# First batch of a retention, Fourier and MLP kernel: part of its transforms from float32 to float16 pairs, with a new order written out by hand

## The chip, the cores and the metric

The kernel runs on one core of one Trainium2 chip. The metric is the device time of one execution in microseconds. Before the change it is 596.29 us, the median of 3 runs (596.05 to 597.14).

## What is computed

The reference chains three blocks over x of 2 batches, 768 tokens and 512 features. The first is a retention (linear attention with decay) over 8 heads. The second adds a Fourier mix and an MLP, the third a plain MLP:

```python
X = np.fft.fft(np.fft.fft(x, axis=1), axis=2)          # over tokens, then over features
u = x + np.real(X)
un = (u - mean(u)) / np.sqrt(var(u) + 1e-06)
y = u + np.maximum(un @ w_ch1, 0.0) @ w_ch2            # 512 -> 2048 -> 512
z = y + np.maximum((norm(y) * g_ln) @ w2_ch1, 0.0) @ w2_ch2
```

Inputs and output are float32, but for the weight matrices, which are float64 and unpacked on the chip.

## The kernel before, in words

The two Fourier transforms are matrix products. Symmetry in tokens and features is used first: rows are added to and subtracted from their mirror rows ("folds"), so that a transform needs about a quarter of the products. Tokens lie in tiles `U[b][j]` of 128 tokens and 512 features, j from 0 to 2 for the first half of the sequence and 3 to 5 for its mirror.

Most products are done in float16 pairs: a float32 number is held as a high and a low float16, and a product is three passes (high by high, high by low, low by high: `PASS`). A pair costs a cast on ScalarE for the high half and a subtraction on GpSimd or VectorE for the low half. In the first batch both transforms are kept in float32, which needs no such pair.

The program has four stages. The retention of batch 0 (0 to about 34 us), its transforms, and the normalization and first tiles of the first MLP (34 to about 67 us) are the head. After that the first MLP runs over four blocks of 384 tokens, with batch 1's retention and transforms and the unpacking of weights in the background, and then the second MLP.

The head from 34 us on is ordered by hand. The string `ORDER` is a list of tokens, each one step of a chain of instructions, and the list is emitted in that order on TensorE, VectorE, ScalarE and GpSimd. The tokens that matter here:
- `k0` to `k2`, `j0` to `j2` are the even and odd folds of tile 0, 1, 2 (`fold_half`, L500 to L517, on VectorE);
- `d<m><g>` is the product of fold m with group g of the first transform (`dft1_mm`), of five groups, accumulated over m = 2, 1, 0; `D<g>` takes a group out of PSUM (`dft1_out`, L543);
- `q<j>`, `p<j>` are the sine and the cosine part of the second transform of tile j (`dft2_q`, `dft2_p`); `X<j>` subtracts and adds the sine part (`sub_sin`, L601), `P<j>` adds the cosine part (`add_cos`, L608);
- `R` is a special row: three GpSimd folds, a cast, and a low half on GpSimd (`row_fold`, L418);
- `b<j>`, `n<j>` are the statistics of the normalization and the normalized, transposed tile (`ln_steps`, `ln_pe_steps`); `M<j><f>` is the first MLP product of tile j and output tile f (f = 0 to 2);
- `c<i>` unpacks weight tile i of the first MLP matrix (`conv_steps`, L286); `W<n>` issues n products whose result is not used.

Unpacking a weight tile takes, on the usual path, a ScalarE copy into `top` (L305), a shift on VectorE (L307), an OR on VectorE (L308), a cast to the high half on ScalarE (L321) and a subtraction for the low half on GpSimd (L323). A second path (L296 to L299) uses two ScalarE copies and one VectorE instruction.

After the hand-ordered part a scheduler orders everything. It may put nothing of the following unpacking on VectorE before the last `n` step there: `after("dve", ...)`, L988 to L993. The shifts L307 of that unpacking write to the PSUM buffers that the second transform's results held, so they also need the last reader of those results on ScalarE (`dft2_yp`, L635 and L636). The names of a tile in the rows leave out buffer numbers: `w` is a weight tile, `f` a fold, `ps_h` and `ps_y` the MLP's sums.

Of the kernel before, what the change touches and what calls it, by code (L numbers as in the profile page):

```python
# [19 lines left out]
P = 128  # L20
# [24 lines left out]
c0 S B1 B0 s s B1 B0 s s O4 B1 B0 O4 c0 I O4 R I O5 O5 O5 O5 c0 c1 c2 W12 k2 j2 k2 k2 d24 d20 d21 j2 j2 d22 d23  # L45
k1 k1 k1 d14 d10 d11 j1 j1 j1 d12 d13 c3 j0 j0 j0 d03 k0 k0 k0 d02 c1 D3 R c2 R c0 D2 d04 d01 D4 d00 c3 D1 q0 D0 q0
c1 q2 q2 X0 X0 q1 q1 c2 X1 p0 p1 P0 c1 X1 P1 b0 b1 b0 X2 c3 p2 c2 b0 b1 X2 P2 c3 b0 n0 b1 b2 b1
W27 n0 b2 n1 n0 b2 W6 n1 n0 b2 M00 n2 n1 n2 n2 n1 M01 M12 M11 M10 n2 M22 M20 M02 M21
# [30 lines left out]
def shape_tables():  # L79
    t = np.arange(TB)  # L80
    s = np.arange(NS)
    ang = 2.0 * np.pi * ((t[:, None] * s[None, :]) % S) / S
    cs = np.cos(ang) * TS
    sn = np.sin(ang) * TS
    d = np.arange(P)
    dd = np.arange(ND)
    cd = np.cos(2.0 * np.pi * ((d[:, None] * dd[None, :]) % DM) / DM) * TS
    dse, dso = d[:, None] * dd[None, 2:-1:2], (d[:, None] + 1) * dd[None, 1::2]
    sd = np.sin(2.0 * np.pi * (np.concatenate([dso, dse], 1) % DM) / DM) * TS
    sd[P - 1, :P] *= 0.5  # L90
# [8 lines left out]
    cdp = np.concatenate([cd[:, ::2], cd[:, 1::2]], 1)  # L99
    drow = np.where(dd[::2] % 4, -0.5, 0.5) * TS  # L100
# [7 lines left out]
    return {  # L108
        "cs": lay(cs, 3),
        "sn": lay(sn[:, :TB], 3),  # L110
        "cd": lay(np.concatenate([cd[:, ::2], cd[:, 1::2]], 1), 1)[:, :, 0],
        "sd": lay(sd, 1)[:, :, 0],
        "cr": ((np.where(s % 2, -1.0, 1.0) - 1.0) * TS).astype(np.float16)[None],
        "dr": (np.where(dd[::2] % 4, -0.5, 0.5) * TS).astype(np.float16)[None],
        "cs32": full(cs, 3),
        "sn32": full(sn[:, :TB], 3),
        "cd32": full(cdp, 1)[:, 0],
        "sd32": full(sd, 1)[:, 0],
        "dr32": drow.astype(np.float32)[None],
        "expo": expo,  # L120
    }
# [3 lines left out]
def tile_retention_fourier_mlp(ctx: ExitStack, tc: tile.TileContext, a: dict, out: bass.AP):  # L125
# [98 lines left out]
    def load_tables(b):  # L224
        if b == 0:
            both = const.tile([P, 2 * ND - 2], F32, tag="big3", name="cdsd32")
            cd, sd = both[:, :ND], both[:, ND:]
            rooms = (("cs", [P, 3, NS], "big1"), ("sn", [P, 3, TB], "big2"), ("cd", cd, None), ("sd", sd, None),
                     ("cr", [1, NS], "cr"), ("dr", [1, NE1], "dr32"))
        else:  # L230
            both = const.tile([P, 2, 2 * ND - 2], F16, tag="big3", name="cdsd")
            cd, sd = both[:, :, :ND], both[:, :, ND:]
            rooms = (("cs", [P, 2, 3, NS], "big1"), ("sn", [P, 2, 3, TB], "big2"), ("cd", cd, None), ("sd", sd, None),
                     ("dr", [1, NE1], "dr"))
        for nm, shape, room in rooms:
            src = nm if b or nm == "cr" else nm + "32"
            tab[nm] = const.tile(shape, F16 if src == nm else F32, tag=room, name=f"{nm}_{b}") if room else shape
            sp.dma_start(tab[nm], a[src])
# [47 lines left out]
    def conv_steps(kind, m, i, which=None, into=None):  # L286
# [6 lines left out]
        if m == 1:  # L293
# [207 lines left out]
    def fold_half(b, m, cos, eng=dve):  # L501
        x_, y_ = U[b][m], U[b][3 + m]
        if (b, m) not in folds:
            folds[b, m] = [f32t(f"{nm}{b}_{m}", 13 - 3 * m + i if b == 0 else None) for i, nm in enumerate("eof")]
            fhl[b, m] = hl(f"fhl{b}_{m}") if b else folds[b, m][2]
# [22 lines left out]
    def dft1_mm(b, g, m, ps, first, last):  # L528
        c0, w, tn, n = GRP[g]
        t = tab[tn]  # L530
        f = fhl[b, m]
        if b == 0:
# [10 lines left out]
    def dft1_out(b, g, ps):  # L543
        w, n = GRP[g][1], GRP[g][3]
        if b == 0:
            t = cst[b, g] = csp.tile([P, NS], F32, tag=f"cs{g}", name=f"cst{b}_{g}")
            act.activation(t[:w, :n], ps[:w, :n], AF.Copy, scale=CS)
            yield
            return
# [6 lines left out]
    def dft1_part(b, g, m, ps):  # L556
        cosg = GRP[g][2] == "cs"
        dft1_mm(b, g, m, ps, m == 2, m == 0 and not cosg)
        if cosg and m == 0:
            dft1_row(b, g, ps)  # L560
# [7 lines left out]
    def dft2_p(b, ps, s0, w):  # L568
        for g, o in ((0, slice(0, NE1)), (1, slice(NE1, ND))):
            if b == 0:  # L570
                pe.matmul(ps[:w, o], cst[b, g][:, s0:s0 + w], tab["cd"][:, o], start=True, stop=g == 1)
                if g == 0:
                    pe.matmul(ps[:w, o], cst[b, 4][0:1, s0:s0 + w], tab["dr"], start=False, stop=True)
                continue
# [10 lines left out]
    def dft2_q(b, j, bk):  # L585
# [4 lines left out]
        for g, o, w in parts:  # L590
            for n, (x, y) in enumerate(PASS if b else ()):
                pe.matmul(ps[:, ND + o:ND + o + w], cst[b, g][:, x, j * P:(j + 1) * P], tab["sd"][:, y, o:o + w],
                          start=n == 0, stop=n == 2)
            if b == 0:
                pe.matmul(ps[:, ND + o:ND + o + w], cst[b, g][:, j * P:(j + 1) * P], tab["sd"][:, o:o + w], start=True, stop=True)
# [97 lines left out]
    def ln_pe_steps(m, blk, j, bk):  # L693
# [10 lines left out]
        act.copy(t[:, 0], psv)  # L704
# [254 lines left out]
    for i in range(NE, 4):  # L959
        chains[f"c{i}"] = lambda i=i: conv_steps(1, 0, i, None if i else "at")  # L960
    for j in range(3):
# [125 lines left out]
    for n in range(total + LAG):  # L1087
# [5 lines left out]
        for _, _, task in sorted(bg.pop(n, ()), key=lambda z: z[0]):  # L1093
            after("dve", task) if n < GATEN else task()
# [30 lines left out]
```

## Time and profile before

| | |
|---|---|
| median of 3 runs | 596.29 us (596.05 to 597.14) |
| the profiled execution | 598.83 us, span 597.0 us |
| TensorE busy | 572.3 us, 96% |
| VectorE busy | 396.0 us, 66% |
| ScalarE, GpSimd busy | 277.4 us (46%), 279.3 us (47%) |
| moved by DMA | 63.23 MB |

The span is what the profile's rows cover, and the execution's time has 1.83 us around it. PE is TensorE, PEld its weight loads, DVE VectorE, ACT ScalarE, POOL GpSimd, SP SyncE, which issues transfers. A busy PE is not PE at its peak, since instructions overlap in its pipeline. The granted clock (PEclk) reads 1.00 at 2.4 GHz and 0.50 at 1.2 GHz.

### The profile page before, as it was taken

To read this page: it belongs to the slowest core of one execution; us is meant where nothing else is said; L and a number is where in the kernel's file an instruction comes from. 1 tells how busy PE (TensorE), PEld (TensorE's weight loads), DVE (VectorE), ACT (ScalarE), POOL (GpSimd) and SP (SyncE) were. 2 spreads that over 40 slices of the span, in tenths; PEclk is the share of its full clock that TensorE was granted. 3 is DMA by queue.
4 is the path that set the end of the run, shared out by engine and by line. 5 is a ranking of instruction groups with operands and counts; after the bars stand their busy time and mean duration, and the time that the engine had idled before them with its cause. 6 is when DMAs were issued, how large, how long until landed. Compare 5 with 4: busy or idle time off the path is not lost. (4 is left out here: it accounts for less than half of the span.)

```text
span 597.0 us, 11805 instructions
## 1 busy us (share of the span) xinstructions
PE 572.3 (96%) x4629; PEld 375.9 (63%) x4629; DVE 396.0 (66%) x869; ACT 277.4 (46%) x557; POOL 279.3 (47%) x294
## 2 busy tenths in 40 slices
PE   7889999989999999999998999999999999999997
PEld 4746645555644554677766666676777677767773
DVE  6897898764695599886597559666545553555333
ACT  3646789643223433454478786864223222322110
POOL 8926889966353575442359776764111200110000
PEclk9999999999999999999999999999999999999999
DMA  8994269842000110353154552510210025002001
GB/s 285 410 414 167 89 201 345 271 154 72 1 1 0 24 31 1 85 146 124 37 163 142 173 175 91 167 27 2 63 27 19 1 85 58 19 1 87 21 2 53
DMA packets 46327, 63.23 MB, mean 106 GB/s; under 512 B 26177, under 2 KB 28351, under 8 KB 46271
## 3 DMA queue, kind: packets, MB, share of 16 engines
q1 hardware_dynamic: 45598, 62.40, 33.0%
q8 instruction: 36, 0.59, 0.4%
q10 hardware_dynamic: 672, 0.08, 0.1%
q14 instruction: 21, 0.16, 0.1%
HBM read 52.23 MB, written 6.29 MB: 98 GB/s over the span
## 5 line engine op out<-in xcount | busy, mean ns | idle before, releaser
L866 PE MATMUL ps_y<-w,h 128*128 128x512 f16 x1152 | 280.6, 380 | 3.4 <-ACT h L851 1.5
L866 PEld LDWEIGHTS <-h 128*128 128x128 f16 x1152 | 109.4, 98 | 105.4 <-issue 4.2
L819 PEld LDWEIGHTS <-sw 128*128 128x128 f16 x1104 | 94.4, 98 | 15.8 <-issue 1.9
L819 PE MATMUL ps<-th,sw 128*128 128x192 f16 x828 | 92.1, 246 | 1.6 <-DVE wf L299 1.3
L323 POOL TENSOR_TENSOR w<-wf,w 128x512 f16<-128x512 f32 x58 | 67.8, 1176 | 39.1 <-ACT w L321 38.9
L819 PEld LDWEIGHTS <-w 128*128 128x128 f16 x828 | 71.9, 98 | 19.0 <-issue 0.6
L851 ACT ACTIVATE h<-ps 128x384 f16<-128x384 f32 x92 | 43.5, 490 | 69.5 <-DVE ps L845 65.8
L726 PE MATMUL ps_h<-unT,w 128*128 128x384 f16 x396 | 73.7, 326 | 1.7 <-DVE h L741 1.6
L819 PE MATMUL ps<-unT,w 128*128 128x192 f16 x552 | 62.7, 246 | 0.0
L726 PEld LDWEIGHTS <-w 128*128 128x128 f16 x396 | 37.0, 98 | 29.8 <-issue 3.1
L852 DVE SCALAR_TENSOR_TENSOR h<-ps,h 128x384 f16<-128x384 f32 x92 | 49.0, 553 | 8.3 <-ACT h L851 6.7
L771 POOL TENSOR_TENSOR sw<-ws,sw 128x512 f16<-128x512 f32 x32 | 38.0, 1198 | 32.8 <-ACT sw L770 32.8
L839 DVE TENSOR_TENSOR t<-ps,s 128x192 f32<-128x192 f32 x46 | 16.3, 355 | 49.6 <-PE ps L819 49.5
L831 ACT COPY s<-ps 128x192 f32<-128x192 f32 x46 | 14.5, 316 | 69.9 <-PE ps L819 69.9
L689 POOL TENSOR_TENSOR uns<-un,uns 128x512 f16<-128x512 f32 x21 | 24.6, 1171 | 41.2 <-ACT uns L688 41.2
L795 POOL TENSOR_TENSOR th<-ts,th 128x384 f16<-128x384 f32 x24 | 22.5, 956 | 36.6 <-ACT th L794 36.6
L321 ACT CAST w<-wf 128x512 f16<-128x512 f32 x58 | 35.1, 612 | 9.8 <-DVE wf L308 6.7
L845 DVE TENSOR_TENSOR ps<-ps,s 128x192 f32<-128x192 f32 x46 | 16.6, 362 | 29.2 <-PE ps L819 28.9
L668 POOL TENSOR_TENSOR rs<-rs,neghalf 128x1 f32<-128x1 f32 x24 | 13.1, 548 | 48.0 <-DVE rs L666 48.0
L832 DVE TENSOR_TENSOR s<-ps,s 128x192 f32<-128x192 f32 x46 | 16.2, 352 | 25.6 <-ACT s L831 25.5
L373 POOL TENSOR_TENSOR m<-m,m 128x512 f16<-128x512 f32 x24 | 31.1, 1310 | 2.5 <-ACT m L371 2.5
L299 DVE SCALAR_TENSOR_TENSOR wf<-ws,ps_w 128x512 int32<-128x512 int32 x32 | 21.9, 683 | 15.1 <-ACT ps_w L297 8.3
(166 smaller groups left out, 847.5 us busy)
## 6 DMA issues: line engine op xcount, KB each, us to landing
ws<-in_w SPq DMA_DIRECT2D x25, 511.8 KB, 4.5
ws<-in_w2b SPq DMA_DIRECT2D x16, 511.8 KB, 3.6
ws<-in_w1b SPq DMA_DIRECT2D x16, 511.8 KB, 4.5
kt<-in_kt SPq DMA_DIRECT2D x12, 256.0 KB, 3.6
qt<-in_qt SPq DMA_DIRECT2D x12, 256.0 KB, 5.2
v<-in_v SPq DMA_DIRECT2D x12, 256.0 KB
k<-in_k SPq DMA_DIRECT2D x12, 256.0 KB, 5.7
pre<-in_w SPq DMA_DIRECT2D x4, 511.8 KB
```

What stands on the lines that cost most here:

```text
L299: dve.scalar_tensor_tensor(ti, raw[:, :, 0], 13, part.bitcast(I32), op0=ALU.logical_shift_right, op1=ALU.bitwise_or)
L321: act.copy(hi, t)
L323: (dve if m == 0 and i in (LD1 if kind == 1 else LD2) else pool).tensor_tensor(lo, t, hi, op=ALU.subtract)
L373: pool.tensor_tensor(t[:, 1], m32, t[:, 0], op=ALU.subtract)
L689: pool.tensor_tensor(s_[:, 1], un, s_[:, 0], op=ALU.subtract)
L726: pe.matmul(ps, w[:, i, k, fo:fo + P], x[:, j, k, :], start=n == 0, stop=n == 11)
L771: pool.tensor_tensor(lo, z, hi, op=ALU.subtract)
L795: pool.tensor_tensor(t[:, 1], z, t[:, 0], op=ALU.subtract)
L819: pe.matmul(ps, lhs, rhs, start=start and n == 0, stop=n == 5, skip_group_check=True)
L851: act.activation(hi, z, AF.Relu)
L852: dve.scalar_tensor_tensor(lo, z, 0.0, hi, op0=ALU.max, op1=ALU.subtract)
L866: pe.matmul(dn[blk][j], h[:, x, j * P:(j + 1) * P], w[:, y], start=f == 0 and n == 0, stop=f == NF - 1 and n == 2)
```

## The change

In batch 0, the last third of the first transform (m = 0) and the whole second transform are done in float16 pairs. The fold of m = 0 gets a pair (a new step `H`), its first two passes are issued first and the third as a step of its own (`l<g>`), `D<g>` makes a pair with a new VectorE instruction, and `q` and `p` take three passes. The tables of the second transform are loaded once, in float16, for both batches. Weight tiles 1 to 3 take the unpacking path with two ScalarE copies. The first subtraction of `X1` moves to GpSimd. The `W27` and `W6` become one `W8`. The unpacking behind the head must wait for the last `n` step on ScalarE as well as on VectorE. `ORDER` is new from the folds on.

```diff
 ORDER = """
-k1 k1 k1 d14 d10 d11 j1 j1 j1 d12 d13 c3 j0 j0 j0 d03 k0 k0 k0 d02 c1 D3 R c2 R c0 D2 d04 d01 D4 d00 c3 D1 q0 D0 q0
+k1 k1 k1 d14 d10 d11 j1 j1 j1 d12 d13 j0 j0 j0 k0 k0 k0 H H c1 c2 c3 c1 c2 c3 d03 d02 d04 d01 d00 l3 D3 D3 l2 D2 D2 l4 D4 D4
...
+        for nm, t in (("cs", cs), ("sn", sn)):
+            tab[nm + "32"] = t
+            sp.dma_start(t[:, 1:], a[nm + "32"][:, 1:])
+            t = tab[nm] = t[:, 0].bitcast(F16).rearrange("p (y n) -> p y n", y=2).unsqueeze(2)
+            sp.dma_start(t[:, :, 0], a[nm][:, :, 0])
...
-        if m == 1:
+        if m == 1 or (kind == 1 and i in (1, 2, 3)):
...
+    def fold_split(b, m):
+        f, t = folds[b, m][2], fhl[b, m]
+        act.copy(t[:, 0], f)
+        yield
+        pool.tensor_tensor(t[:, 1], f, t[:, 0], op=ALU.subtract)
+        yield
...
-    def dft1_mm(b, g, m, ps, first, last):
+    def dft1_mm(b, g, m, ps, first, last, part=slice(0, 3)):
...
-        if b == 0:
-            pe.matmul(ps[:w, :n], f[:, c0:c0 + w], t[:, m, :n], start=first, stop=last)
+        if b == 0 and m > 0:
+            pe.matmul(ps[:w, :n], f[:, c0:c0 + w], tab[tn + "32"][:, m, :n], start=first, stop=last)
             return
-        for i, (x, y) in enumerate(PASS):
-            pe.matmul(ps[:w, :n], f[:, x, c0:c0 + w], t[:, y, m, :n], start=first and i == 0, stop=last and i == 2)
+        for i, (x, y) in enumerate(PASS[part]):
+            pe.matmul(ps[:w, :n], f[:, x, c0:c0 + w], tab[tn][:, y, m, :n], start=first and i == 0,
+                      stop=last and part.start + i == 2)
...
-            for n, (x, y) in enumerate(PASS if b else ()):
+            for n, (x, y) in enumerate(PASS):
...
-        dve.tensor_tensor(x_[:, :ND], x_[:, :ND], qs, op=ALU.subtract)
+        (eng if j == 1 else dve).tensor_tensor(x_[:, :ND], x_[:, :ND], qs, op=ALU.subtract)
...
-        act.copy(t[:, 0], psv)
+        gate["act"] = act.copy(t[:, 0], psv)
...
-    after("dve", lambda: [w_conv(2, 0, i) for i in range(2)])
+    after("dve", lambda: after("act", lambda: [w_conv(2, 0, i) for i in range(2)]))
```

Two places show what the new order does. The first is GpSimd, from the special row's low half (`rhl`) to the powers of the normalization (`rs`). `w` is the low half of weight tile 0, 1, 2, 3 in turn, `u` with `qs` a step of `X`, `fhl` the fold's new low half. Line numbers are those of each kernel. Before:

```order
L431 TENSOR_TENSOR rhl_763<-r_653,rhl_763 1x257
L323 TENSOR_TENSOR w_0_0_688<-wf_0_0_578,w_0_0_688 128x512
L323 TENSOR_TENSOR w_0_0_688<-wf_0_1_690,w_0_0_688 128x512
L605 TENSOR_TENSOR u_119<-u_119,qs_198 128x255
L323 TENSOR_TENSOR w_0_0_688<-wf_0_2_692,w_0_0_688 128x512
L605 TENSOR_TENSOR u_119<-u_119,qs_199 128x255
L323 TENSOR_TENSOR w_0_0_688<-wf_0_3_744,w_0_0_688 128x512
L668 TENSOR_TENSOR rs_0_0_832<-rs_0_0_832,neghalf 128x1
```

With the change:

```order
L429 TENSOR_TENSOR rhl_720<-r_655,rhl_720 1x257
L321 TENSOR_TENSOR w_0_0_690<-wf_0_0_580,w_0_0_690 128x512
L521 TENSOR_TENSOR fhl_0_764<-f_0_763,fhl_0_764 128x512
L321 TENSOR_TENSOR w_0_0_690<-wf_0_1_705,w_0_0_690 128x512
L321 TENSOR_TENSOR w_0_0_690<-wf_0_2_710,w_0_0_690 128x512
L321 TENSOR_TENSOR w_0_0_690<-wf_0_3_715,w_0_0_690 128x512
L594 TENSOR_TENSOR u_119<-u_119,qs_198 128x257
L596 TENSOR_TENSOR u_119<-u_119,qs_198 128x255
L659 TENSOR_TENSOR rs_0_0_873<-rs_0_0_873,neghalf 128x1
```

The first two instructions are the same, but the cast that feeds `rhl` now stands on ScalarE ahead of the fold's cast, where before it stood behind the first group taken out of PSUM. The four low halves stand together, and both steps of `X1` follow them on GpSimd.

The second place is ScalarE at the end of the head, from the last transposed tile (`unT`, from `ps_l`) to the first high half of the unpacking behind it (`w`). `cosy` are the cosine results, read out of the PSUM buffers `ps_pq` 0, 1, 2. Before:

```order
L635 ACTIVATE cosy_0_1064<-ps_pq_0_786 128x129
L636 ACTIVATE cosy_0_1064<-ps_pq_0_786 128x128
L635 ACTIVATE cosy_1_1075<-ps_pq_1_801 128x129
L636 ACTIVATE cosy_1_1075<-ps_pq_1_801 128x128
L635 ACTIVATE cosy_2_1080<-ps_pq_2_794 128x129
L636 ACTIVATE cosy_2_1080<-ps_pq_2_794 128x128
L704 CAST unT_0_841<-ps_l_0_2_922 128x4x128
L740 ACTIVATE h_0_0_1030<-ps_h_0_0_905 128x384
L321 CAST w_0_0_1051<-wf_0_0_1046 128x512
```

With the change:

```order
L695 CAST unT_0_887<-ps_l_0_2_1000 128x4x128
L303 ACTIVATE top_189<-ws_0_0_1071 128x512
L303 ACTIVATE top_190<-ws_0_1_1081 128x512
L626 ACTIVATE cosy_0_1091<-ps_pq_0_818 128x129
L627 ACTIVATE cosy_0_1091<-ps_pq_0_818 128x128
L626 ACTIVATE cosy_1_1107<-ps_pq_1_825 128x129
L627 ACTIVATE cosy_1_1107<-ps_pq_1_825 128x128
L626 ACTIVATE cosy_2_1112<-ps_pq_2_832 128x129
L627 ACTIVATE cosy_2_1112<-ps_pq_2_832 128x128
L303 ACTIVATE top_188<-pre_344 128x512
```

The readers of the second transform's buffers stood ahead of the last transposed tile and now stand behind it, with two `top` copies between. Before, those two copies stood far ahead, among the groups of the first transform.

## Rows read from the trace of the kernel before

**Rows 1.** Windows: stretch, length, busy us (instructions) of PE, PEld, DVE, ACT, POOL, PEclk, DMA share, GB/s.

```profile
60.00:70.00 10.00, 8.85 (x123) 7.00 (x121) 7.84 (x15) 6.82 (x18) 8.14 (x11) 1.00 0.29 106
70.00:80.00 10.00, 8.86 (x49) 4.54 (x48) 10.00 (x22) 7.68 (x17) 7.76 (x8) 1.00 0.31 80
80.00:90.00 10.00, 10.00 (x64) 5.50 (x62) 9.80 (x20) 9.91 (x19) 10.00 (x11) 1.00 0.83 258
...
110.00:120.00 10.00, 9.79 (x107) 6.00 (x107) 8.43 (x16) 6.39 (x12) 9.90 (x10) 1.00 0.87 294
120.00:140.00 20.00, 17.63 (x147) 9.95 (x145) 11.80 (x19) 9.09 (x17) 13.03 (x12) 0.91 0.43 136
```

**Rows 2.** Timeline, folds to unpacking: start us, us, engine, line, operation, count, [idle before <-releaser].

```profile
35.98 0.61 ACT L321 CAST w<-wf 128x512 f16<-128x512 f32 x1
...
40.74 0.68 DVE L507 TENSOR_TENSOR o<-u 128x512 f32<-128x512 f32 x1
...
43.72 0.29 DVE L513 TENSOR_TENSOR f<-e 128x129 f32<-128x129 f32 x1
...
45.49 0.67 POOL L431 TENSOR_TENSOR rhl<-r,rhl 1x257 f16<-1x257 f32 x1 [10.78 <-DVE wf L307]
45.58 2.24 DVE L308 TENSOR_TENSOR wf<-wf,top 128x512 int32<-128x512 int32 x1
...
46.12 1.15 POOL L323 TENSOR_TENSOR w<-wf,w 128x512 f16<-128x512 f32 x1
```

**Rows 3.** Timeline, TensorE: the end of the first transform, and the first MLP products.

```profile
42.49 2.74 PE L533 MATMUL ps_d<-sn,f 128*128 128x384 f32 x8
...
48.58 0.50 PE L541 MATMUL ps_d<-cr,rhl 1*128 1x385 f16 x2
...
61.74 5.52 PE L716 MATMUL ps_h<-unT,w 128*128 128x128 f16 x96
```

**Rows 4.** Timeline, second transform to the first shift of the unpacking behind the head.

```profile
50.48 0.43 DVE L603 TENSOR_TENSOR u<-u,qs 128x257 f32<-128x257 f32 x1 [1.53 <-ACT qs L598]
...
52.46 1.40 DVE L613 SCALAR_TENSOR_TENSOR u<-ps_pq,u 128x256 f32<-128x256 f32 x4
...
53.79 1.27 DVE L660 BATCH_NORM_STATS2 bst<-u 128x6 f32<-128x512 f32 x2
...
55.07 1.26 DVE L603 TENSOR_TENSOR u<-u,qs 128x257 f32<-128x257 f32 x1
...
58.16 0.66 PE L701 MATMUL ps_l<-expo,un 128*128 128x128 f32 x4 [1.14 <-ACT un L680]
...
61.57 0.29 ACT L635 ACTIVATE cosy<-ps_pq 128x129 f32<-128x129 f32 x1
...
63.80 1.28 DVE L307 TENSOR_SCALAR ps_w<-ws 128x512 int32<-128x512 int32 x2
```

**Rows 5.** Timeline, the first weight tile behind the head, and TensorE behind it.

```profile
65.58 1.88 DVE L308 TENSOR_TENSOR wf<-ps_w,top 128x512 int32<-128x512 int32 x3
65.96 0.49 ACT L740 ACTIVATE h<-ps_h 128x384 f16<-128x384 f32 x1 [2.80 <-PE ps_h L716]
...
67.04 1.16 POOL L323 TENSOR_TENSOR w<-wf,w 128x512 f16<-128x512 f32 x1 [1.22 <-ACT w L321]
...
69.62 0.55 DVE L741 SCALAR_TENSOR_TENSOR h<-ps_h,h 128x384 f16<-128x384 f32 x1
...
78.76 2.11 PE L726 MATMUL ps_h<-unT,w 128*128 128x384 f16 x12
...
80.71 2.11 PE L866 MATMUL ps_y<-w,h 128*128 128x512 f16 x9
```

**Rows 6.** Timeline of the late stall.

```profile
123.90 0.66 ACT L296 ACTIVATE half<-ws 128x512 f16<-128x512 bf16 x1 [3.48 <-DMA ws<-in_w2b]
...
129.82 0.58 PE L476 MATMUL ps_st<-vhl,khl 128*64 128x64 f16 x24 [1.29 <-DVE int L409]
```

**Rows 7.** Window behind that stall (columns as in rows 1).

```profile
132.00:134.00 2.00, 2.00 (x7) 0.71 (x6) 1.93 (x5) 0.62 (x1) 1.26 (x2) 0.50 0.75 244
```

More of the change, by code (lines that the diff above doesn't have):

```diff
@@ L116, in shape_tables @@
         "sn32": full(sn[:, :TB], 3),
-        "cd32": full(cdp, 1)[:, 0],
-        "sd32": full(sd, 1)[:, 0],
-        "dr32": drow.astype(np.float32)[None],
         "expo": expo,
@@ L224, in load_tables @@
     def load_tables(b):
-        if b == 0:
[L226 to L238, printed above, removed]
+        cs, sn = (const.tile([P, 3, n], F32, tag=f"big{i}", name=f"{nm}_{b}") for i, nm, n in ((1, "cs", NS), (2, "sn", TB)))
+        if b:
+            for nm, t in (("cs", cs), ("sn", sn)):
+                t = tab[nm] = t.rearrange("p k n -> p (k n)").bitcast(F16).rearrange("p (y k n) -> p y k n", y=2, k=3)
+                sp.dma_start(t, a[nm])
+            return
+        for nm, t in (("cs", cs), ("sn", sn)):
+            tab[nm + "32"] = t
+            sp.dma_start(t[:, 1:], a[nm + "32"][:, 1:])
+            t = tab[nm] = t[:, 0].bitcast(F16).rearrange("p (y n) -> p y n", y=2).unsqueeze(2)
+            sp.dma_start(t[:, :, 0], a[nm][:, :, 0])
+        both = const.tile([P, 2, 2 * ND - 2], F16, tag="big3", name="cdsd")
+        tab["cd"], tab["sd"] = both[:, :, :ND], both[:, :, ND:]
+        tab["cr"] = const.tile([1, NS], F16, name="cr")
+        tab["dr"] = const.tile([1, NE1], F16, name="dr")
+        for nm in ("cd", "sd", "cr", "dr"):
+            sp.dma_start(tab[nm], a[nm])
     neghalf = const.tile([P, 1], F32, name="neghalf")
@@ L504, in fold_half @@
             folds[b, m] = [f32t(f"{nm}{b}_{m}", 13 - 3 * m + i if b == 0 else None) for i, nm in enumerate("eof")]
-            fhl[b, m] = hl(f"fhl{b}_{m}") if b else folds[b, m][2]
+            fhl[b, m] = hl(f"fhl{b}_{m}") if b or m == 0 else folds[b, m][2]
         z, f = folds[b, m][1 - cos], folds[b, m][2]
@@ L554, in dft1_out, with dft1_part @@
         yield
-    def dft1_part(b, g, m, ps):
+    def dft1_part(b, g, m, ps, part=slice(0, 3)):
         cosg = GRP[g][2] == "cs"
-        dft1_mm(b, g, m, ps, m == 2, m == 0 and not cosg)
-        if cosg and m == 0:
+        dft1_mm(b, g, m, ps, m == 2, m == 0 and not cosg, part)
+        if cosg and m == 0 and part.stop == 3:
             dft1_row(b, g, ps)
@@ L569, in dft2_p @@
         for g, o in ((0, slice(0, NE1)), (1, slice(NE1, ND))):
[L570 to L574, printed above, removed]
             for n, (x, y) in enumerate(PASS):
@@ L965, in tile_retention_fourier_mlp @@
         chains[f"n{j}"] = lambda j=j: ln_pe_steps(0, 0, j, bk0)
+    chains["H"] = lambda: fold_split(0, 0)
     todo = {"S": lambda: attn_scores(0, 5, bk0)}
+    todo |= {f"l{g}": lambda g=g: dft1_part(0, g, 0, ps1[g], slice(2, 3)) for g in range(5)}
     todo |= {f"d{m}{g}": lambda m=m, g=g: first(g, m) for m in range(3) for g in range(5)}
@@ L997, in tile_retention_fourier_mlp @@
         after("pool", lambda: dft2_y0(0, j))
-    after("dve", lambda: [w_conv(2, 0, i) for i in range(2)])
+    after("dve", lambda: after("act", lambda: [w_conv(2, 0, i) for i in range(2)]))
     for j in range(3):
-        dft2_y(0, j, bk0) if YA[0] == "a" else after("dve", lambda: dft2_y(0, j, bk0))
+        after("act", lambda: dft2_y(0, j, bk0)) if YA[0] == "a" else after("dve", lambda: dft2_y(0, j, bk0))
     NB = 2 * B
@@ L1093, in tile_retention_fourier_mlp @@
         for _, _, task in sorted(bg.pop(n, ()), key=lambda z: z[0]):
-            after("dve", task) if n < GATEN else task()
+            after("dve", lambda: after("act", task)) if n < GATEN else task()
         if n >= LAG:
```

25 lines of the change are left out of this document (6 added, 19 removed).

## The prediction

> **What bounds the kernel now.** I read the windows first, then the timeline of the head, then the waits of the stages behind it. The windows show who is full in which stage [rows 1]. From 70 to 80 us VectorE is busy 10.00 of 10 us and TensorE 8.86: there the unpacking of the MLP's weights sets the pace. From 80 to 90 TensorE is busy 10.00 and so on to 118 us, with 9.79 between 110 and 120. What is still lost behind that lies mostly between 120 and 140 us (17.63 of 20, and a mean granted clock of 0.91). So a change of the head is worth what it does to the moment from which TensorE has no gap, and that moment hangs on the first unpacking instruction behind the head, VectorE's shift at 63.80 us [rows 4]. In the timeline the reader is to see what that shift waits for, which is where the change bites.
>
> **The change, part by part.** I follow the chain from the last fold to that shift.
>
> *Folds.* They end at 44.01 us now (43.72 + 0.29), and GpSimd was idle for 10.78 us before its step on the special row at 45.49 [rows 2]. In the new order this step needs only a ScalarE cast that stands ahead of the fold's cast. ScalarE starts its weight cast at 35.98 (0.61), then has three pairs of copies. The first of a pair took 0.66 [rows 6], the second has no row in the head, and I price it as the cast, 0.61 [rows 2]; three pairs are 3.8 us, so GpSimd starts at about 40.7. Its two instructions (0.67 and 1.15) then run until 42.5, in the middle of the folds, where VectorE works on SBUF operands without a pause (the fold at 40.74 took 0.68). The one place where the trace has such a meeting is 45.58: a VectorE instruction of that size, both inputs in SBUF, took 2.24 us beside exactly these two GpSimd instructions, so 1.56 more than 0.68 [rows 2]. I take 1.6 (bounds 0, if they don't meet, and 1.8, both GpSimd instructions whole). The last fold is then ready at 45.6.
>
> The Trainium skill, "SBUF — State Buffer", section "SBUF: two separate sides", says that VectorE with two SBUF inputs and GpSimd exclude each other for whole instructions. By that rule the term would be 1.8 instead of 1.6 and the sum 0.2 us higher; the measured row decides here.
>
> *First transform, last third.* A float32 product of 384 columns took 0.69 (2.74 for eight records, two to a product) [rows 3]; in float16 twelve of them start 1.95 apart from the next group, so 0.16 each [rows 5], and three passes are 0.49. TensorE gains 0.2 on each of five groups, but first waits for the new cast, 0.61 behind the last fold. Cast done at 46.2; ten products of the first two passes, 1.6; five third passes, 0.8; six products on the special row, 0.215 each (0.43 for the two before 49.01, where the sine part begins), 1.3. The new low half (1.15 on GpSimd) is ready at 47.4, behind the ten products' start and ahead of their end at 47.8, so it costs nothing; if the cover went, it would cost up to 1.15. The transform ends at 49.9, where it was 49.0 now [rows 3].
>
> *Second transform.* The last group leaves PSUM as a pair: by the nearest rows 0.49 on ScalarE and 0.55 on VectorE [rows 5], done at 51.1 with the hand-overs. The sine subtractions of tile 0 are two of 0.43 [rows 4]; now GpSimd does the first half of tile 1 beside them. Such a meeting stretched the same line to 1.26 at 55.07, 0.83 more. I take 0.6 (bounds 0 and 0.83), since a GpSimd instruction of half of 1.15's length is the partner here. Two cosine additions are 0.7 (1.40 for four) [rows 4]: done at 53.3. The sine and cosine products run in this time on TensorE and cost nothing. From the last addition to the first transposes now pass 4.3 us (53.86 to 58.16). I take off the 0.83 of stretch and one of the two statistics (0.64), and add the two additions that the new order puts in between (0.7): 3.5. First transposes at 56.8, **1.3 us earlier than now**.
>
> *To the shift.* The third tile's statistics now stand behind the first tile's low half: 56.8 + 0.66 + a cast 0.61 + 0.69 is 58.8. From statistics to transposes took 4.37 (53.79 to 58.16), less 0.83 and 0.64, so 2.9, and the second tile's low half stands in between, 0.7: third transposes at 62.4, where the trace before shows the last of the tiles done before the shift at 63.80 [rows 4]. Behind them ScalarE has the transposed tile's cast (0.66 + 0.1 + 0.61: 63.8), then two weight copies (0.66 each by rows 6: 65.1), and only then the two readers of the PSUM buffer that the first shift writes (0.29 each, overlapping: 0.46) [rows 4]. **The shift starts at 65.5 instead of 63.80: 1.7 us later.** The removed warm-up products, 33 against 8, were not on this chain.
>
> *Behind the shift.* From the first shift to the first low half in place are 63.80 to 68.20 now [rows 4, 5], so 69.9 then. TensorE's first tiles end earlier than now: 63.1 after the third transposes plus half of the 96 products that took 5.52 [rows 3] is 66, against 67.26. That gain is hidden: TensorE waits for the weights in either case, and VectorE is full behind the shift. So I carry the 1.7 us to 80.71, from where TensorE has no gap [rows 5], and to the end.
>
> *Edits at no cost.* Tiles 1 to 3 need one VectorE instruction instead of two; these stand where VectorE waits for TensorE. Two more table transfers, equal bytes: the folds cover them, and ScalarE reads the weights behind them only from 36.6 on; uncovered they cost two issues of SP. The second transform's tables are not loaded again later: nothing waited for them. The added wait on ScalarE is in the chain above.
>
> **Sum.** The profiled execution takes 598.83 us (span 597.0 and 1.83 around it), and 600.5 with 1.7 more. The median of the runs is 2.54 below the profiled one, so 596.29 + 1.7 = **598.0 us**. A measurement of this kernel can tell about 0.2%, 1.2 us, from no change. With the bounds of the two meetings the forecast's own range is 597.0 to 599.0.
>
> **The rivals.**
>
> *The two engines don't meet* (no change). If GpSimd's steps fall between folds, or wait until the folds are done, and tile 1's half doesn't hold up tile 0's, 1.6 + 0.6 go: the shift at 63.3, 0.5 earlier than now, 595.8 us. For it: the new order does shorten the chain to the transposes. Against it: two meetings in the trace, both with a stretch [rows 2, 4].
>
> *The clock falls* (slower still). With 8 warm-up products for 33, TensorE stands from about 66 to 69.9 with one product in between. At 129.82 it had stood for 1.29 us, worked 0.58 and stood again, and from 132 to 134 the granted clock was 0.50, 1.2 GHz [rows 6, 7]. Two microseconds at half clock are 1.0 lost, the whole drop 1.8 (0.09 of 20 us) [rows 1]. VectorE then waits for the products of output tile 3, so the loss would be passed on: 599.0 to 599.8. It decides if the gap is as long as worked out. The Trainium skill, "TensorE: Matmul & The Clock Gate", Part 1, says that the throttled state is the default and that only activity releases it; by that rule this rival is what happens, and the trace agrees with its 0.50 behind the gap.
>
> *The late stall closes* (faster). Between 120 and 140 us the loss is 2.4 us of idle TensorE and 1.8 of clock, 4.2 together [rows 1]. It comes from one place: ScalarE stood for 3.48 us in front of a weight transfer of the second MLP, with the retention's casts queued behind it [rows 6]. The scheduler gave this stage another order, with one of those copies moved among the casts. If the transfer lands before ScalarE gets there, most of it goes: 598.0 - 3.7 = 594.3. Against it: the transfers hang on the buffers that the same unpacking frees, and that starts later.
>
> **How the numbers follow.** The forecast has 0.40, no meeting 0.20, the clock 0.22, the closed stall 0.18. The range reaches from the closed stall to the clock's upper end, 594.0 to 600.0; about 0.15 is left for the full stall saved on top of the missing meetings and for losses in sum above the clock's. Slower by over 0.2%: the clock and most of the forecast, 0.22 + 0.35 = 0.57. Within 0.2%: no meeting, but for a little, and the forecast's lower end, 0.22. Faster by over 0.2%: the closed stall and what is left, 0.21.
>
> **What would show it.** Right: GpSimd's low half of the special row at about 41 us with a fold beside it of well over 0.68; the last fold at 45.6; the first transposes before 57.5; the first shift behind the head after 65, released by ScalarE's cosine readers; TensorE idle for over 2 us behind the first tiles. Wrong: folds that end at 44.0, a shift before 64.2, or a stretch from 120 to 140 us with TensorE full. A granted clock under 1.00 between 66 and 75 us is the second rival.

## The result, and the profile after

The changed kernel takes 603.21 us (median of 6 runs, 601.32 to 606.13) against 596.51 for the kernel before on the same chip (6 runs): a ratio of 1.0111, 95% interval 1.0091 to 1.0132. It is slower by 6.7 us, where 1.7 were forecast, and lies outside the range (594.0 to 600.0).

| | before | after |
|---|---|---|
| the profiled execution, span | 598.83, 597.0 us | 603.88, 602.1 us |
| last fold ends | 44.01 | 45.49 |
| first, third transposes | 58.16, 61.25 | 56.78, 63.57 |
| first shift behind the head | 63.80 | 66.44 |
| first product on a weight tile from behind the head | 67.10 | 69.61 |
| mean granted clock | 0.996 | 0.993 |

The profiled executions differ by 5.05 us, the medians by 6.7: that of the kernel before lost 1.8 us to the clock behind its late stop [rows 1, 7], which its executions at a mean clock of 0.999 or 1.000 (60 of the 107 in the comparisons below, 594.4 to 597.1 us) didn't lose.

Windows after, columns as in [rows 1]; the lines from 60:70 to 120:140 answer to those:

```profile
58.00:60.00 2.00, 1.89 (x16) 1.81 (x16) 1.63 (x4) 0.77 (x2) 0.13 (x1) 0.59 0.00 0
60.00:62.00 2.00, 2.00 (x22) 1.93 (x21) 0.88 (x2) 0.74 (x2) 2.00 (x4) 0.56 0.00 0
...
60.00:70.00 10.00, 7.56 (x104) 6.87 (x102) 5.13 (x10) 7.08 (x17) 7.65 (x12) 0.91 0.17 54
70.00:80.00 10.00, 8.80 (x52) 4.45 (x52) 10.00 (x21) 7.77 (x16) 7.91 (x8) 1.00 0.17 53
80.00:90.00 10.00, 10.00 (x56) 5.17 (x54) 10.00 (x20) 9.32 (x17) 9.97 (x11) 1.00 0.80 250
110.00:120.00 10.00, 10.00 (x90) 6.11 (x89) 7.02 (x11) 7.69 (x13) 8.92 (x10) 1.00 0.79 290
120.00:140.00 20.00, 17.49 (x171) 10.38 (x170) 14.40 (x25) 9.61 (x18) 13.29 (x13) 0.92 0.57 183
...
220.00:240.00 20.00, 18.73 (x102) 9.86 (x101) 19.19 (x42) 6.55 (x13) 12.29 (x13) 1.00 0.15 14
240.00:260.00 20.00, 17.92 (x130) 11.48 (x129) 15.06 (x33) 9.78 (x19) 8.65 (x10) 1.00 0.33 86
```

The same two late windows of the kernel before, not shown so far:

```profile
220.00:240.00 20.00, 18.38 (x99) 9.53 (x98) 18.04 (x38) 7.65 (x16) 11.80 (x13) 1.00 0.05 10
240.00:260.00 20.00, 20.00 (x156) 13.54 (x155) 17.28 (x37) 9.26 (x18) 7.12 (x7) 1.00 0.44 114
```

Two things meet the eye. The clock falls in the head: the granted share is 0.59 and 0.56 from 58 to 62 us. And far behind the head, where the diff touches nothing, TensorE is idle for 1.27 + 2.08 = 3.35 us between 220 and 260, before for 1.62. The stop between 120 and 140 us is as large as it was.

Timeline after, from the folds to the first warm-up products, which answers to [rows 2, 3]:

```profile
40.56 0.69 POOL L429 TENSOR_TENSOR rhl<-r,rhl 1x257 f16<-1x257 f32 x1 [5.96 <-ACT rhl L427]
40.64 2.27 DVE L505 TENSOR_TENSOR o<-u 128x512 f32<-128x512 f32 x1
41.22 1.14 POOL L321 TENSOR_TENSOR w<-wf,w 128x512 f16<-128x512 f32 x1
...
45.20 0.29 DVE L511 TENSOR_TENSOR f<-e 128x129 f32<-128x129 f32 x1
...
45.52 0.62 ACT L519 CAST fhl<-f 128x512 f16<-128x512 f32 x1 [5.04 <-DVE f L511]
...
46.20 0.82 PE L538 MATMUL ps_d<-sn,fhl 128*128 128x384 f16 x4 [2.35 <-ACT fhl L519]
...
50.10 0.49 PE L544 MATMUL ps_d<-cr,rhl 1*128 1x385 f16 x2
...
51.95 1.02 POOL L594 TENSOR_TENSOR u<-u,qs 128x257 f32<-128x257 f32 x1 [1.23 <-ACT qs L589]
51.97 0.42 DVE L596 TENSOR_TENSOR u<-u,qs 128x255 f32<-128x255 f32 x1
...
52.53 0.76 DVE L604 SCALAR_TENSOR_TENSOR u<-ps_pq,u 128x256 f32<-128x256 f32 x2
...
53.65 1.04 PE L975 MATMUL warm<-expo 128*128 128x256 f16 x8
```

The fold beside GpSimd's step takes 2.27 instead of 0.68, and TensorE stands for 2.35 us in front of the float16 products, where it had float32 work before. In the second meeting, at 51.95, it is GpSimd's step that is stretched (1.02; its next one takes 0.72), and VectorE's takes 0.42.

Timeline after, from the first transposes to the first tiles' end, which answers to [rows 4, 5]:

```profile
56.78 0.66 PE L692 MATMUL ps_l<-expo,un 128*128 128x128 f32 x4 [2.10 <-ACT un L671]
...
58.70 0.69 DVE L651 BATCH_NORM_STATS2 bst<-u 128x6 f32<-128x512 f32 x1
...
60.07 3.66 PE L707 MATMUL ps_h<-unT,w 128*128 128x128 f16 x48
...
61.84 0.82 ACT L671 ACTIVATE un<-u,rs 128x512 f32<-128x512 f32 x1 [0.95 <-DVE rs L670]
...
64.69 1.42 ACT L303 ACTIVATE top<-ws 128x512 f16<-128x512 bf16 x2
...
65.95 0.28 ACT L626 ACTIVATE cosy<-ps_pq 128x129 f32<-128x129 f32 x1
...
66.44 1.29 DVE L305 TENSOR_SCALAR ps_w<-ws 128x512 int32<-128x512 int32 x2 [0.92 <-ACT cosy L627]
...
69.61 0.59 PE L857 MATMUL ps_y<-w,h 128*128 128x512 f16 x2 [2.31 <-ACT w L319]
```

The shift is released by the cosine readers, as forecast. The third tile is ready for its transposes at 62.66, but they start at 63.57: 48 products stand ahead of them on TensorE, and at the low clock these take 3.66 us.

### The profile page after: what moved, and what is told of

It is laid out like the page before. It is cut to its first block, busy times and chain, and to the rows that moved or that the text cites. A ratio compares the mean times of both kernels' runs of the same rounds, so it can differ in the third digit from the quotient of the medians.

```text
span 602.1 us, 11797 instructions
## 1 busy us (share of the span) xinstructions
PE 570.1 (95%) x4623; PEld 374.1 (62%) x4623; DVE 397.1 (66%) x869; ACT 281.2 (47%) x561; POOL 281.4 (47%) x297
## 5 line engine op out<-in xcount | busy, mean ns | idle before, releaser
L830 DVE TENSOR_TENSOR t<-ps,s 128x192 f32<-128x192 f32 x46 | 16.3, 355 | 50.0 <-PE ps L810 49.9
L297 DVE SCALAR_TENSOR_TENSOR wf<-ws,ps_w 128x512 int32<-128x512 int32 x34 | 23.2, 684 | 15.1 <-ACT ps_w L295 8.3
L810 PE MATMUL ps<-th,w 128*128 128x192 f16 x276 | 31.0, 246 | 0.4 <-DVE t L830 0.4
```

Of the source, the lines that this page charges most:

```text
L297: dve.scalar_tensor_tensor(ti, raw[:, :, 0], 13, part.bitcast(I32), op0=ALU.logical_shift_right, op1=ALU.bitwise_or)
L810: pe.matmul(ps, lhs, rhs, start=start and n == 0, stop=n == 5, skip_group_check=True)
```

## The experiments

Of every run the table has the median of its executions, the ratio to the kernel before on the same chip with its 95% interval, and, of the one execution that was profiled, its time, the start of the first shift behind the head, and TensorE's idle time in three stretches (us). A profiled execution can lie some us from the median, so its last four columns belong to the profiled time.

| run | median | ratio | profiled | shift | 60:80 | 100:140 | 220:260 |
|---|---|---|---|---|---|---|---|
| before | 596.51 | 1 | 598.83 | 63.80 | 2.29 | 2.58 | 1.62 |
| the change | 603.21 | 1.0111 (1.0091 to 1.0132) | 603.88 | 66.44 | 3.64 | 3.05 | 3.35 |
| f16, old order | 599.20 | 1.0042 (1.0029 to 1.0054) | 599.35 | 67.46 | 1.91 | 0.83 | 1.61 |
| f32, new order | 602.76 | 1.0091 (1.0065 to 1.0117) | 599.61 | 65.35 | 2.43 | 2.29 | 3.34 |
| warm-ups 27 and 6 | 602.33 | 1.0100 (1.0077 to 1.0123) | 606.95 | 70.71 | 2.57 | 2.66 | 3.35 |
| 19 more | 601.25 | 1.0085 (1.0058 to 1.0112) | 600.60 | 67.38 | 2.58 | 1.25 | 3.35 |
| f16, old order, 10 more | 600.61 | 1.0067 (1.0046 to 1.0088) | 600.52 | 67.00 | 2.48 | 0.97 | 1.61 |
| the change again | 603.89 | 1.0118 (1.0093 to 1.0143) | 604.01 | 68.68 | 3.12 | 2.80 | 3.36 |
| before again (one run) | 598.28 | | 598.28 | 63.97 | 2.30 | 1.91 | 1.62 |
| row late | 602.08 | 1.0093 (1.0072 to 1.0113) | 603.25 | 67.95 | 3.51 | 1.84 | 3.34 |
| cosine readers free | 602.80 | 1.0096 (1.0066 to 1.0125) | 602.89 | 68.05 | 3.18 | 2.33 | 3.35 |
| statistics early | 604.35 | 1.0130 (1.0110 to 1.0151) | 603.96 | 67.91 | 3.70 | 2.24 | 3.34 |
| cosine readers in order | 602.05 | 1.0106 (1.0065 to 1.0147) | 603.42 | 65.67 | 2.72 | 3.58 | 3.34 |
| last line | 597.08 | 1.0012 (0.9999 to 1.0025) | 595.77 | 64.65 | 1.24 | 1.73 | 1.72 |
| 8 behind | 599.53 | 1.0044 (1.0027 to 1.0062) | 597.88 | 66.81 | 2.63 | 1.42 | 1.70 |
| 2 behind | 599.87 | 1.0048 (1.0029 to 1.0068) | 600.09 | 66.69 | 3.37 | 2.09 | 1.92 |
| 20 behind | 601.95 | 1.0075 (1.0049 to 1.0102) | 599.91 | 66.55 | 2.44 | 0.04 | 3.11 |
| undone together | 596.28 | 0.9985 (0.9969 to 1.0001) | 597.59 | 64.76 | 1.13 | 1.51 | 1.71 |
| further, f16 | 596.35 | 0.9996 (0.9981 to 1.0010) | 597.18 | 63.23 | 0.83 | 1.45 | 1.94 |
| further, f32 | 596.11 | 0.9995 (0.9981 to 1.0009) | 597.08 | 63.84 | 0.82 | 0.71 | 3.35 |

### Pairs or order

```diff
 f16, old order: the code of the pairs, and
-... c3 j0 j0 j0 d03 k0 k0 k0 d02 c1 D3 R c2 R c0 D2 d04 d01 D4 d00 c3 D1 q0 D0 q0
+... c3 j0 j0 j0 k0 k0 k0 H H d03 d02 c1 R c2 R c0 d04 d01 d00 l3 D3 D3 l2 D2 D2 l4 D4 D4 c3 l1 D1 D1 q0 l0 D0 D0 q0
 f32, new order: the new ORDER without H and l
```

> The float16 pairs of the change alone, in the order of the kernel before (its unpacking path, its warm-ups, its X1 on VectorE and GpSimd, no wait on ScalarE); the order behind the head is that of the kernel before. If the new order carries the loss: first shift between 63.5 and 64.5 us, median 596 to 597.5. If the pairs or their split table transfers carry it: first shift at 65.5 or later, median over 600.

> The new order alone, with the first batch's transforms left in float32 (its unpacking path, its 8 warm-ups, X1 on GpSimd, the wait on ScalarE). If the new order carries the loss: first shift at about 66 us, a drop of the granted clock near 58 us, median 602 to 604. If the pairs carry it: first shift before 64.5, median under 598. Theory B is wrong if the median follows the shift in this run and in the one with the pairs alone; it holds if a kernel with an early shift is at 600 or more.

The new order alone gives 602.76, all but the whole loss; with the pairs in it, it is 603.21, and the intervals overlap. The pairs alone give 599.20, with a shift at 67.46, so neither case of the first expectation holds: the steps of the pairs aren't free in an order that wasn't made for them. But the shift doesn't tell the time: of the two profiled executions, the one with its shift at 67.46 took 599.35 us and the one with 65.35 took 599.61. And in the profile of the new order the clock fell at 70 us, behind a stop of 2.31, not near 58 as expected.

### The clock

```diff
 warm-ups 27 and 6:
-W8 n0 n0 P2 n1 n0 M00 ...
+W27 n0 n0 P2 n1 n0 W6 M00 ...
 19 more: that, and
-... c1 c2 c3 c1 c2 c3 d03 ...
+... c1 c2 c3 c1 c2 c3 W19 d03 ...
 f16, old order, 10 more:
-... D1 D1 q0 l0 ...
+... D1 D1 W10 q0 l0 ...
```

> The changed kernel with the 27 and 6 warm-up products of the kernel before in place of the 8; nothing else in the order of any engine differs. Theory A (what counts is when the first shift behind the head starts, and half clock from 58 to 62 us kept TensorE's queue from the third transposes): granted clock 1.00 from 54 to 70 us, third transposes at about 62.7 instead of 63.52, first shift at about 65.6 instead of 66.44, median about 602.4 against 603.2. Theory B (the loss sits behind the head, in the stalls from 100 us on, and does not hang on the shift): median 603.2 whatever the shift does.

> The changed kernel with 19 warm-up products ahead of the first float16 product of the fold of tile 0 (where TensorE stood for 2.35 us), and 27 and 6 in place of the 8: TensorE stands for over 1 us nowhere between 36 and 66 us. If the stops let the clock fall: granted clock 1.00 from 40 to 66 us, third transposes at about 62.7 instead of 63.52, first shift at about 65.6 instead of 66.44 (70.71 with the 27 and 6 alone), median 601.5 to 602.4. If the clock falls for another reason: 0.50 somewhere between 46 and 62 us in spite of the filling, and a median of 603 or more. Either way 1.7 us of the loss stay, since the order behind the head is all but that of the changed kernel: TensorE idle for over 3 us between 220 and 260.

> The pairs in the old order with ten warm-up products ahead of the first sine products of the second transform, where TensorE stood for 1.35 us (48.66 to 50.00) and the clock was at 0.50 from 50 to 60 in the run without them. Nothing behind the head moves. If that stop let the clock fall: granted clock 1.00 from 44 to 66 us, first transposes at about 59 instead of 61.43, first shift at about 64.8 instead of 67.46, median 596.7 to 597.5 instead of 599.2. If the clock falls because float16 products load TensorE otherwise, whatever the stops: 0.50 again between 48 and 60, median about 599.

> The changed kernel once more, unaltered. If the clock falls by chance behind the same stops: the granted clock at 0.50 in other places between 46 and 75 us than from 58 to 62, the instructions the same; median 601.5 to 604.

In the profile with 27 and 6 the clock fell earlier, and its shift at 70.71 is that of the slowest of its seven executions (606.95). The first two windows are of the change and of this run, the third of this run:

```profile
48.00:50.00 2.00, 2.00 (x11) 0.56 (x8) 1.07 (x3) 1.38 (x4) 2.00 (x3) 1.00 1.04 409
...
48.00:50.00 2.00, 2.00 (x7) 0.61 (x6) 0.27 (x1) 0.79 (x2) 2.00 (x3) 0.50 1.03 400
...
58.00:60.00 2.00, 2.00 (x12) 1.50 (x11) 2.00 (x6) 0.43 (x1) 1.36 (x2) 0.50 0.00 0
```

Up to 53 us its instructions are those of the change, whose clock was at 1.00 there. So behind the same stop the clock falls in some executions: in 4 of the 11 profiles that have a stop of 2.30 to 2.36 us there (the change again among them, 0.50 from 47 to 50 and from 61 to 64). That it is chance is not shown: three of the four had lost the clock once before, at 9 us, and none of the other seven had. Behind the second stop, of 2.1 us and more in front of the first transposes, it fell in all ten profiles with 8 warm-up products in the new float16 order.

The 19 products did not fill the first stop. Timeline of that run:

```profile
46.12 2.25 PE L975 MATMUL warm<-expo 128*128 128x256 f16 x19 [2.30 <-DVE wf L297]
...
61.83 2.84 PE L707 MATMUL ps_h<-unT,w 128*128 128x128 f16 x48
```

They waited themselves for a PSUM buffer of the unpacking and put everything 2 us back. Still the clock stayed at 1.00 from 40 to 71 us, and the 48 products took 2.84 instead of 3.66. The median is 2 us lower, with a shift 0.94 later, but the intervals overlap. In the old order the expectation was wrong: the clock fell all the same (55 to 59 us, without the filling 50 to 60), the shift moved by only 0.46, and the median is 1.4 higher, again with intervals that overlap.

### The steps of the head, one by one

```diff
 row late:
-... W12 c1 c2 c3 R R c0 k2 ... k0 k0 k0 H H c1 ...
+... W12 c1 c2 c3 k2 ... k0 k0 k0 H H R R c0 c1 ...
 statistics early:
-... P2 n1 n0 M00 b2 b2 b2 b2 n1 M01 n1 n1 M02 n2 M10 M11 n2 n2 n2 ...
+... P2 n1 b2 b2 b2 b2 n0 M00 n1 M01 n2 n1 n1 M02 n2 M10 M11 n2 n2 ...
 cosine readers free (in order: three new tokens behind M01 as well):
-after("act", lambda: dft2_y(0, j, bk0)) if YA[0] == "a"
+dft2_y(0, j, bk0) if YA[0] == "a"
```

> The changed kernel with the cast and the low half of the special row and weight tile 0's low half moved on ScalarE and GpSimd from ahead of the folds of tile 1 to behind the last fold. Theory A: no VectorE fold over 0.7 us, last fold at about 43.9 instead of 45.49, first transposes at about 55.2 instead of 56.78, first shift at about 64.9 instead of 66.44, median about 601.6. Rival: the same two GpSimd instructions then meet the three VectorE steps of the weight tiles and the fold's own low half, and the chain gets nothing: first transposes at 56.3 or later, median about 603.

> The changed kernel without the wait of the cosine readers on ScalarE's last cast: they stand ahead of the third transposed tile's cast again, the two top copies stay behind it. If these readers are what the first shift waits for: the shift is released by VectorE's own low half instead, at about 65.5 instead of 66.44 at the same clock, median about 602.3. Rival: VectorE's OR then waits for the top copies, and the first low half stays at 70.8, median 603.

> The changed kernel with the third tile's three VectorE statistics steps and its normalization moved ahead of the first and the second tile's low half and cast; the cosine readers stay behind the last cast, and the order behind the head is that of the change to the instruction. If the later first shift is the loss: shift about 1 us earlier, 65.4 instead of 66.44, and a median about 1 us lower, 602.2 to 602.8, with both moves together 601. If the order behind the head holds the larger part: 601 or more here, and no median of 597 by these moves alone; TensorE still idle for 3.3 us between 220 and 260 and for over 1 us between 76 and 80.

> The changed kernel with the cosine readers written into ScalarE's order ahead of the second tile's cast, and nothing else; the order behind the head is that of the change but for one cast and one VectorE step. First shift released by VectorE's third low half, at about 65.5 instead of 66.44; TensorE's wait of 2.3 us for the first weight tile about 1 us shorter; median 602 to 603. If 597 to 598 comes out, the cosine readers were the whole loss.

With the row late, no fold takes over 0.69 us and the last one ends at 44.39. The gain is lost at once. Its timeline:

```profile
48.09 0.69 DVE L297 SCALAR_TENSOR_TENSOR wf<-pre,ps_w 128x512 int32<-128x512 int32 x1 [2.51 <-POOL w L321]
...
49.33 1.96 ACT L549 ACTIVATE cst<-ps_d 128x384 f16<-128x384 f32 x5
```

Weight tile 3 waits for the buffer that tile 0's low half frees, its cast waits on ScalarE, and the first group behind that cast leaves PSUM at 49.33. The cosine readers do release the shift earlier: in the run with them in the order it starts at 65.67, right behind VectorE's third low half. In the other three the clock was lost earlier than in the change, and their shifts come at 67.9 and later, where 64.9 to 65.5 were expected. None of the four moves the median by over 1.2 us, all their intervals overlap with that of the change, and the loss between 220 and 260 us stays at 3.34 or 3.35 in all.

### The order behind the head

```diff
 last line: the cosine readers, and the statistics early, together
 2, 8, 20 behind:
-... M20 M21 M22
+... M20 M21 M22 W8
```

> The changed kernel with the last line of its order alone undone: the third tile's statistics ahead of the first tile's low half, its normalization ahead of the second tile's cast, and the cosine readers written ahead of both. Special row, weight tiles and the 8 warm-up products stay as in the change. If these steps carry half of the delay: first transposes as in the change (56.8 us), third transposes at about 61.5 instead of 63.57, first shift at about 63.8 to 64.3 instead of 66.44, median about 600. If the steps ahead of the first transposes or the clock carry it: first shift at 65.5 or later, median 602 or more.

> The changed kernel with eight warm-up products behind the last product of its head (0.9 us within a stop of 2.3); the order behind the head is another, with the normalization step that stood ahead of the MLP's sums at 236 us behind them. If the order behind the head holds most of the loss: first shift at 66.4 as in the change (later where the clock falls), TensorE idle for about 1.7 between 220 and 260 instead of 3.35 and for less between 67 and 80, median 598 to 600. If the head holds it: 602 or more.

> The same with two such products (0.2 us). The order behind the head differs less from that of the change, but the normalization step is behind the sums too. If that one step is what counts: TensorE idle for 1.7 between 220 and 260, median 1.7 below the change, 601.5 to 602. If the head holds the loss: 603.

> The same with twenty (2.2 us, all of the stop). If the order behind the head holds most of the loss: 597.5 to 600, with no fall of the clock between 66 and 75 us. If the head holds it: 602 or more.

> The kernel before once more, unaltered. If the loss of the clock from 132 to 134 us comes in some executions only: an execution of 595.5 to 596.5 without it, with the stop of TensorE at 129 to 131 us there or shorter; if it comes always: 598 with it.

With the last line undone, 597.08, below the 600 expected, though the shift (64.65) is later than forecast. One by one its two parts leave 602 to 604; together they also make the scheduler order all that follows in another way. The traces show it, by comparing VectorE's 755 instructions from the first shift on by name and shape: 37 of them stand elsewhere than in the change, and with one part alone at most 1. The change and the eight other runs with its order there (0 to 3 elsewhere) take 601.3 to 604.4, whatever their head. Two or eight products without use behind the last product of the head change that order alone (19 and 32 elsewhere) and take 3.3 and 3.7 us off, with the first shift where it was; of two, 1.7 were expected if one step alone counted. The run with eight, first its shift and the eight products, then three windows:

```profile
66.81 1.29 DVE L305 TENSOR_SCALAR ps_w<-ws 128x512 int32<-128x512 int32 x2 [0.92 <-ACT cosy L627]
...
69.98 0.59 PE L857 MATMUL ps_y<-w,h 128*128 128x512 f16 x2 [2.31 <-ACT w L319]
...
70.41 1.04 PE L975 MATMUL warm<-expo 128*128 128x256 f16 x8
```

```profile
120.00:140.00 20.00, 18.74 (x193) 11.61 (x192) 14.59 (x24) 10.09 (x19) 15.34 (x15) 1.00 0.59 185
220.00:240.00 20.00, 18.30 (x100) 9.61 (x99) 18.04 (x37) 8.16 (x16) 11.60 (x12) 1.00 0.07 12
240.00:260.00 20.00, 20.00 (x158) 13.63 (x157) 17.18 (x40) 8.80 (x18) 6.18 (x6) 1.00 0.47 124
```

This profiled execution is the fastest of its twelve, so its span, 596.1, is 6.0 below that of the change, where the medians differ by 3.7. Of the 6.0, 1.01 lie between 60 and 80 us, 1.63 between 100 and 140 and 1.65 between 220 and 260 (by the table), and 1.6 are the clock between 120 and 140 (0.92 against 1.00): 5.9 in sum, with smaller differences of either sign elsewhere (between 40 and 60 us it stands 0.44 longer). The products didn't fill the stop they were meant for (TensorE still stood for 2.31 us; they ran at 70.41, behind it), so it is not their filling that helps. With twenty, 601.95, no gain is shown (the interval overlaps with that of the change), against the expectation: 33 instructions stand elsewhere, TensorE is idle for 0.04 between 100 and 140 but for 3.11 between 220 and 260. Another order is not a better one everywhere, and which of the moved instructions count is open.

What such a difference looks like, in the change at 236 us (VectorE, then TensorE):

```profile
234.99 1.31 DVE L776 TENSOR_TENSOR ts<-tr,ts 128x192 f32<-128x192 f32 x1
236.22 1.10 DVE L670 SCALAR_TENSOR_TENSOR rs<-mv,rs 128x1 f32<-128x1 f32 x1
237.25 0.54 DVE L732 SCALAR_TENSOR_TENSOR h<-ps_h,h 128x384 f16<-128x384 f32 x1
...
237.85 2.11 PE L717 MATMUL ps_h<-unT,w 128*128 128x384 f16 x12 [1.27 <-DVE h L732]
```

A step of one element per partition stands ahead of the step `h` that TensorE waits for, and takes 1.10 us on a VectorE without a pause. In the orders with 1.6 to 1.9 us there (before, last line, 2 and 8 behind) it is behind `h`. That it isn't the only thing that counts is shown by the last run of the table: 3.35 us there, and 596.11.

The kernel before, profiled again, lost the clock behind its late stop again (598.28 us at a mean clock of 0.994). So a profile without that loss is missing. It doesn't come in every execution: the 60 of 107 at a mean clock of 0.999 or 1.000 have a median of 596.0, the 31 at 0.996 or 0.997 one of 597.5.

### Undone together

```diff
+... k0 k0 k0 H R H c0 R c1 c2 c1 c2 W8 d03 ... c1 l1 D1 D1 c3 l0 D0 c2 q0 q1 q2 q0 D0 X0 X0 q1 X1 X1 q2 c3 c3 p0 ...
+W27 n0 n0 P2 n1 b2 b2 b2 b2 n0 W6 M00 n1 M01 n1 n2 n1 M02 n2 M10 M11 n2 n2 M12 M20 M21 M22 W16
 further: without that W8, with W29, the cosine readers written behind M01, and n2 ahead of n1's cast
```

> Float16 pairs with the steps undone together: special row and weight tile 0's low half behind the folds (weight tile 3's VectorE step, cast and low half later still), third tile's statistics ahead of the first tile's low half, cosine readers free, warm-up products in every stop of TensorE over 0.8 us (8, 27, 6, and 16 behind the first tiles). The scheduler also puts the statistics step that stood ahead of the MLP's sums at 236 us back behind them. Theory A with the clock as its second part: last fold at 44.4, granted clock 1.00 up to 80 us, third transposes at about 60.3, first shift at 62.5 to 63, TensorE's idle time between 220 and 260 about 1.7 instead of 3.35: median 597 to 598. If the loss sits elsewhere behind the head: a shift before 64 and still 600 or more.

> The kernel with the steps undone together, further: no warm-up products ahead of the first float16 products (they waited for a PSUM buffer of the unpacking), the third tile's normalization ahead of the second tile's cast on ScalarE, and the cosine readers written into the order where ScalarE idles. Third transposes at about 60.7 instead of 62.70, first shift at 62.7 to 63.2 (63.80 in the kernel before), clock 1.00 up to 80 us: median 594 to 595, faster than both kernels. If the shift is not what counts: 596 or more.

> The same order with the transforms of the first batch in float32, as in the kernel before. If the pairs bring the head nothing by themselves: third transposes within 0.5 us of the run with pairs, median within 1 us of it. If they do shorten the path: third transposes 1 to 2 us later, median 1 to 2 us higher.

All three are as fast as the kernel before, none faster beyond its interval. So 594 to 595 was wrong, though the first shift of that run is 0.57 us earlier than in the kernel before; and the first of the three is as fast with a shift 0.96 later. The last two differ in the pairs, and 596.35 against 596.11 is no difference. But the scheduler gave them two orders (36 VectorE instructions stand elsewhere), so this compares the pairs together with a chance order. Under one order behind the head the pairs cost 2.6 us in the old one (599.20 against 596.58 on the same chip) and nothing that shows in the new one (603.21 against 602.76). In the further order they make the shift 0.61 us earlier (63.23 and 63.84), and TensorE idle for 2.57 us between 40 and 60, where the float32 products leave 0.82.

## Why the prediction was wrong

**Folds, right.** GpSimd's step at 40.56 (forecast 40.7), the fold beside it stretched by 1.59 (1.6), the last fold at 45.49 (45.6).

**The transforms and the first transposes, right by luck.** The first transform ends at 50.59 instead of 49.9: the products start 0.16 to 0.18 us apart only within a group, and 0.25 to 0.27 apart where the operand or the shape changes. The cosine additions still end at 53.29, as forecast (53.3), because the stretch of 0.6 counted for tile 0's sine subtractions didn't come: they took 0.42 each, and it was GpSimd's step beside them that was stretched. Two errors cancel, and the first transposes at 56.78 are the forecast 56.8.

**To the shift, right in mechanism, 0.94 short.** Third transposes at 63.57 instead of 62.4, of which 0.82 is the low clock on 48 products (3.66 against 2.84 at a clock of 1.00). The shift follows by 2.87, forecast 3.1, released by the readers that were named. The second rival had the clock's fall, but behind the first tiles, from 66 us on. It came eight microseconds ahead of that, behind the stop in front of the first transposes (2.10, before 1.14). The warm-up products that had stood there are those that the prediction calls "not on this chain". At the low clock TensorE's queue is the chain, and with 27, 6 and 19 of them the clock held; with 27 and 6 it had fallen before they came.

**The rule on the clock.** "TensorE: Matmul & The Clock Gate" of the Trainium skill, Part 1, has the throttled state as the default, released by activity. The traces show falls behind stops, but not behind each: behind the first stop, of 2.30 to 2.36 us, the granted clock fell in 4 of 11 profiles and stayed in 7, so a stop makes the fall possible and not certain.

**What the clock costs.** At a mean clock of 0.996 or 0.997 three executions of the change took 601.3 to 603.0 (median 602.4), and 31 of the kernel before 594.8 to 598.3 (median 597.5). So about 4.8 of the 6.7 us stay at an equal clock, and some 2 go with it, about what the second rival had (up to 1.8).

**"I carry the 1.7 us to 80.71 ... and to the end", the step that failed.** It takes the work behind the head for the same work in the same order, later. The third rival says that the scheduler gives a stage behind the head another order, and counts only a gain from it. With the head as it is, other orders behind it give 599.5, 599.9 and 602.0 instead of 603.2: up to 3.7 of the 6.7 us are in that order, which the diff doesn't show. It isn't the clock that differs: three executions with 8 behind at 0.996 or 0.997 took 597.9 to 599.1, where the change took 601.3 to 603.0. From 8 behind to the last line the median falls by a further 2.4; the shift there is 2.16 earlier, but 16 VectorE instructions stand elsewhere too, so that this is the head's part is not shown. The remaining 0.6 is within what the comparisons resolve.

**The range.** The bounds of the two meetings, 0 to 1.8 and 0 to 0.83, give 595.8 to 598.4 and not the 597.0 to 599.0 that the prediction names as the forecast's own range. The measured time lies above both.

**The stop between 120 and 140 us** did not close (TensorE busy for 17.49 of 20), so the third rival didn't happen in the change: ScalarE still waits 2.58 us for the transfer (before 3.48). In the run with eight behind it waits 2.77, so there too the rival's mechanism didn't come, though that stretch is fuller (18.74, at a clock of 1.00).

## What to carry to other kernels

If a part of a program is ordered by hand and a scheduler orders the rest from simulated times, an edit of the part changes the rest too: compare the order of the whole before the edit is costed, and test the edit with two or three idle fillers at the seam, so that a chance order is not taken for its worth. Cheaper products in a stretch where TensorE doesn't set the pace opened stops here (2.57 us of idle time against 0.82), and the clock is paid for on the products behind them. Price a stop by who stands in TensorE's queue behind it.

## What the runs showed of the hardware

The same instructions behind the same stop were granted 2.4 GHz in one execution and 1.2 GHz in another, for 3 us (the change again, from 47 to 50) or for 14 (the run with 27 and 6, from 47 to 61), and the slowest of the six executions of the change, 606.1 us, has the lowest mean clock, 0.988 (the others 601.3 to 603.9 at 0.990 to 0.997). A filling product can wait as well: it needs a PSUM buffer, and the 19 stood for 2.30 us for one that VectorE still read.
